# Routing in two rounds through a table in DRAM: a fused attention and mixture-of-experts kernel

## The chip, the core and the metric

The kernel runs on one core of a Trainium2 chip. A core has five engines that run side by side, each through its own queue of instructions in order: PE (TensorE, matrix products into PSUM), DVE (VectorE), ACT (ScalarE), POOL (GpSimd) and SP (SyncE, here only used to issue DMAs). The profile lists PE's weight loads apart, as PEld. The metric is the time of one execution on the device in microseconds (us); lower is better.

## The reference, cut to what matters

`B, H, S, D = 8, 8, 576, 64`; eight experts, model width 512, hidden width 1024, all in f32.

```python
# attention: heads 0-3 see the last 32 positions, heads 4-7 every 32nd position before
scores = where(mask, q @ k.T / sqrt(64), -1e9)
x = softmax(scores) @ v                      # laid out as (B, S, 512)
# mixture of experts, one expert per row
logits = x @ w_gate                          # (B, S, 8)
fresh = argmax(logits); stay = sigmoid(x @ w_local) >= 0.5
for b in range(B):
    for s in range(S):                       # e follows the row before when stay is set
        e = prev_e if (s > 0 and stay[b, s]) else fresh[b, s]
        out[b, s] = softmax(logits[b, s])[e] * (relu(x[b, s] @ w1[e]) @ w2[e])
```

A row can only be put to its expert when its logits are known and the rows before it in its batch have been decided. The order of batches doesn't matter to the result.

## The kernel before

**Attention** (`attention`, L148). The work is cut into 32 pairs of heads (8 batches of 4 pairs, two local and two strided), each pair into two units (`Unit`). One loop, L389, goes over the 64 units: it issues `load` four pairs ahead on SP, `scores` and `mask` of unit n, `values` and `norm` of unit n-2, `store_x` (the finished rows to the DRAM tensor `xd`, by POOL, L305 and L311), `turn_x` of unit n-4, and for the last pair of a batch `logits` and `gates` 5 and 6 units later. `gates` leaves, for each row, its softmax (`probs`) and a code for the expert it picks (`codes`). The order is written out by hand (`manual_schedule`). From unit 12 on the weights of expert 0 are loaded by SP (`Weights.ready`, L577), and from unit 20 on one of 16 sums of weight blocks is formed per unit, by POOL (L582).

**Routing** (`route`, L412) runs once, after all batches. It turns the codes so that each of 64 lines is one (batch, expert), scans along the 576 positions for the expert in force (`last`, L464), counts (`cum`, L472), works out a slot for each row, and then inverts rows to slots by products with one-hot matrices: `at` (L539), `put` (L540 on POOL, L541 on DVE), `lane` (L545) and 96 products into `tab` (L548). From `tab` come `gi` (the row to gather for each slot), `si` (the row to scatter to) and `gate`.

**Experts** (`experts`, L601). Slots come in tiles of 128 rows, up to seven per expert. For every expert in turn two pairs of tiles are always done, and a `Switch` on the count of its tiles runs the rest. A pair is `pair_hidden` (L680, seven products of 16 matmuls, Strassen-like with sums of blocks) and `pair_output` (L716, seven products of 8); `gather` (L629), `scale` (L635), `turn` (L642) and `row_sums` (L651) bring up the next pair while the output of this one is computed; `scatter` (L655) writes the result rows. The weights of expert e+1 are loaded at the start of expert e, and their 16 sums (`steps`) are spread over e's work on DVE.

Of the kernel before, what the change touches and what calls it, by code (L numbers as in the profile page):

```python
# [8 lines left out]
F32 = mybir.dt.float32  # L9
# [9 lines left out]
P = 128  # L19
# [25 lines left out]
NT = E * XT  # L45

AT = (N + E * (P - 1)) // P

# [41 lines left out]
def attention_then_scomoe(ctx: ExitStack, tc: tile.TileContext, qkl, qks, vl, vs, wg, q, k, vl2, vs2, wg2, w1, w2, out):  # L90
# [6 lines left out]
    flag = keep.tile([1, 1], I32, name="flag")  # L97

    with ExitStack() as fast:
        once = fast.enter_context(tc.tile_pool(name="once", bufs=1))  # L100
        gi = once.tile([P, NT], I32, name="gi")
        si = once.tile([P, NT], I32, name="si")
        gate = once.tile([P, NT], F32, name="gate")
        pick = once.tile([1, E], I32, name="pick")
        sums = once.tile([P, 2 * B * PAIRS, 2, 3], F32, name="sums")
        tabs = gi, si, gate, pick, flag
        one = Weights(once)
        with ExitStack() as first:
            routing = first.enter_context(tc.tile_pool(name="routing", bufs=1))
            probs = routing.tile([LQ, LT, B, E], F32, name="probs")  # L110
            codes = routing.tile([LQ, LT, B, E], F32, name="codes")
            with ExitStack() as part:
                with tc.manual_schedule():
                    attention(part, tc, qkl, qks, vl, vs, wg, xd, ident, probs, codes, sums,
                              lambda: one.ready(nc, w1, w2, 0))
            with ExitStack() as part:
                route(part, tc, ident, probs, codes, sums, tabs)
        with ExitStack() as part:
            with tc.manual_schedule():
                experts(part, tc, xd, w1, w2, out, ident, tabs, one)  # L120
# [27 lines left out]
def attention(ctx, tc, qkl, qks, vl, vs, wg, xd, ident, probs, codes, sums, weights):  # L148

    nc = tc.nc  # L150
    consts = ctx.enter_context(tc.tile_pool(name="consts", bufs=1))
# [5 lines left out]
    psS = ctx.enter_context(tc.tile_pool(name="psS", bufs=2, space=PSUM))  # L157
    psV = ctx.enter_context(tc.tile_pool(name="psV", bufs=2, space=PSUM))
    psT = ctx.enter_context(tc.tile_pool(name="psT", bufs=1, space=PSUM))
# [65 lines left out]
    ci = consts.tile([LQ, E], I32, name="ci")  # L225
    nc.gpsimd.iota(ci, pattern=[[-1, E]], base=E, channel_multiplier=0)
    down = consts.tile([LQ, E], F32, name="down")
    nc.vector.tensor_copy(down, ci)
    pi = consts.tile([LQ, LT], I32, name="pi")
    nc.gpsimd.iota(pi, pattern=[[E * LQ, LT]], base=E, channel_multiplier=E)  # L230
    pos8 = consts.tile([LQ, LT], F32, name="pos8")
    nc.vector.tensor_copy(pos8, pi)
    start = consts.tile([LQ, LT], F32, name="start")
# [63 lines left out]
    def store_x(u):  # L297
# [3 lines left out]
        for a in range(2):  # L301
            if u.local:
                w = LQ // 2
                o = dst.rearrange("(t a p) d -> a p t d", a=2, p=w)[a]
                nc.gpsimd.dma_start(out=o, in_=src[a * (P - w):a * (P - w) + w])  # L305
                continue
            for j in range(GT):
# [3 lines left out]
                nc.gpsimd.dma_start(out=o, in_=src[a * (P - w):a * (P - w) + w, j])  # L311
# [39 lines left out]
    def gates(b):  # L351
        ps = psV.tile([P, 2, 3, V1], F32, name="vps").rearrange("p a i e -> p (a i e)")
        lt = ps[0:LQ, 0:LT * (E + 1)].rearrange("p (t e) -> p t e", e=E + 1)
        for t in range(LT):
            nc.tensor.matmul(lt[:, t], lhsT=st["lT", b][:, t * LQ:(t + 1) * LQ], rhs=fold,  # L355
                             start=(t == 0), stop=True, skip_group_check=True)
        lg = lt[:, :, 0:E]
        mx = small.tile([LQ, LT], F32, name="gmx")
        nc.vector.tensor_reduce(mx, lg, axis=AX.X, op=Alu.max)
        mxb = spread(mx, [LQ, LT, E])  # L360
        ex = small.tile([LQ, LT, E], F32, name="ex")
        nc.vector.tensor_tensor(ex, lg, mxb, op=Alu.subtract)

        eq = small.tile([LQ, LT, E], F32, name="eq")
# [22 lines left out]
    for n, u in enumerate(units):  # L387
        u.n = n
# [907 lines left out]
```

## Time and profile before

| | us |
|---|---|
| median of 3 runs (lowest, highest) | 782.3 (781.42, 784.19) |
| the profiled execution: its own time | 780.91 |
| its span | 779.2 |
| PE busy, DVE, ACT, POOL | 707.3, 391.5, 199.1, 173.5 |
| last value product of the attention ends | 167.5 |
| first matmul of the first expert's hidden layer | 239.6 |
| last output scatter ends | 762.6 |

The span is the part of an execution that the profile covers; 1.7 us of the profiled execution's time lie around it. Busy time is the union of an engine's instructions. A row of a group gives the line of the program, the engine, the operation, what it writes and reads, and how often; then the time in total, the mean of one in ns, and idle time of the engine just ahead of it with what ended that idle time. The chain of waits is followed back from the last instruction, at each step to what released it.

### The profile page before, as it was taken

To read this page: it belongs to the slowest core of one execution; us is meant where nothing else is said; L and a number is where in the kernel's file an instruction comes from. 1 tells how busy PE (TensorE), PEld (TensorE's weight loads), DVE (VectorE), ACT (ScalarE), POOL (GpSimd) and SP (SyncE) were. 2 spreads that over 40 slices of the span, in tenths; PEclk is the share of its full clock that TensorE was granted. 3 is DMA by queue.
4 is the path that set the end of the run, shared out by engine and by line. 5 is a ranking of instruction groups with operands and counts; after the bars stand their busy time and mean duration, and the time that the engine had idled before them with its cause. 6 is when DMAs were issued, how large, how long until landed. Compare 5 with 4: busy or idle time off the path is not lost.

```text
span 779.2 us, 15215 instructions
## 1 busy us (share of the span) xinstructions
PE 707.3 (91%) x6244; PEld 638.5 (82%) x6244; DVE 391.5 (50%) x842; ACT 199.1 (26%) x357; POOL 173.5 (22%) x216
## 2 busy tenths in 40 slices
PE   7998899984467999999999999999999999999990
PEld 5887788863467999999899799899989899889990
DVE  6457655537802664366364266466436546333430
ACT  2553344540002222122222222122212222222210
POOL 2346743330210210120121120131012112112101
PEclk9999999995558999999999999999999999999995
DMA  9999678320025110622520712620161432011000
GB/s 332 340 404 306 214 253 268 116 71 1 0 76 196 49 46 18 239 79 76 198 69 30 251 43 60 232 82 29 42 220 55 147 124 70 30 33 56 29 3 23
DMA packets 31639, 95.67 MB, mean 123 GB/s; under 512 B 5614, under 2 KB 5614, under 8 KB 31472
## 3 DMA queue, kind: packets, MB, share of 16 engines
q1 hardware_dynamic: 19424, 64.33, 24.0%
q0 software_dynamic: 11520, 29.39, 11.4%
q8 instruction: 64, 1.05, 0.6%
q14 instruction: 103, 0.84, 0.3%
q10 hardware_dynamic: 528, 0.07, 0.1%
HBM read 74.87 MB, written 19.92 MB: 122 GB/s over the span
## 4 chain that ended last, share of the span: by engine, by line
PE 83%; DVE 6%; issue 5%; ACT 2%; DMA 1%; POOL 1%; ACTq 0%; another core or an unknown queue 0%; POOLq 0%; DVEq 0%
PE mps L716 28%; PE lps L680 28%; PE vps L280 6%; PE sps L256 6%; PE tps L321 3%; PE tab L548 3%; PE xps L642 2%; PE lps L771 2%; PE mps L781 2%; DVE eq L369 1%; PE sps L250 1%; PE tps L340 1%; PE vps L355 1%; DVE put L541 1%; DMA x<-xd,gi 1%
## 5 line engine op out<-in xcount | busy, mean ns | idle before, releaser
L655 POOL DMA_INDIRECT out_dram<-y,si x40 | 47.7, 1192 | 387.2 <-DVE y L668 300.9
L680 PE MATMUL lps<-tt,ws 128*128 128x128 f32 x912 | 108.0, 275 | 0.0
L680 PEld LDWEIGHTS lps<-tt,ws 128*128 128x128 f32 x912 | 104.9, 192 | 0.0
L716 PE MATMUL mps<-wt,k 128*128 128x256 f32 x456 | 101.5, 379 | 0.0
L716 PEld LDWEIGHTS mps<-wt,k 128*128 128x128 f32 x456 | 86.6, 190 | 11.8
L680 PE MATMUL lps<-xt,w1t 128*128 128x128 f32 x608 | 75.5, 278 | 6.1 <-ACT p L687 6.0
L680 PEld LDWEIGHTS lps<-xt,w1t 128*128 128x128 f32 x608 | 73.0, 193 | 9.3 <-ACT p L687 7.5
L716 PE MATMUL mps<-w2t,h 128*128 128x256 f32 x304 | 71.9, 379 | 0.0
L667 ACT ACTIVATE h<-h 128x512 f32<-128x512 f32 x57 | 35.9, 630 | 113.4 <-DVE h L668 113.4
L668 DVE TENSOR_TENSOR h<-lps,u 128x512 f32<-128x512 f32 x57 | 39.4, 691 | 49.9 <-PE lps L680 49.9
L716 PEld LDWEIGHTS mps<-w2t,h 128*128 128x128 f32 x304 | 56.3, 190 | 6.9
L311 POOL DMA_DIRECT2D xd<-xs x80 | 45.7, 576 | 61.4 <-DVE xs L294 47.3
L629 POOL DMA_INDIRECT x<-xd,gi x40 | 39.1, 976 | 85.6 <-issue 39.2
L256 PE MATMUL sps<-qk 64*128 64x96 f32 (+2 forms) x704 | 55.3, 289 | 0.5 <-DMA qk<-in_qkl_dram 0.5
L260 ACT ACTIVATE e<-sps 128x576 f32<-128x576 f32 (+1 forms) x64 | 41.6, 650 | 49.4 <-PE sps L256 49.2
L256 PEld LDWEIGHTS sps<-qk 64*128 64x128 f32 (+2 forms) x704 | 44.7, 188 | 11.1 <-issue 9.3
L668 DVE TENSOR_TENSOR u<-lps,p 128x512 f32<-128x512 f32 x19 | 13.1, 691 | 52.3 <-ACT p L687 20.8
L680 PE MATMUL lps<-tt,w1t 128*128 128x128 f32 x304 | 37.0, 275 | 0.0
L680 PE MATMUL lps<-xt,ws 128*128 128x128 f32 x304 | 37.0, 275 | 0.0
L643 ACT COPY xt<-xps 128x512 f32<-128x512 f32 x40 | 21.7, 589 | 59.6 <-PE xps L642 59.6
L668 DVE TENSOR_TENSOR u<-lps,u 128x512 f32<-128x512 f32 x19 | 13.1, 691 | 45.6 <-PE lps L680 45.6
L716 PE MATMUL mps<-w2t,k 128*128 128x256 f32 x152 | 36.0, 379 | 0.0
(190 smaller groups left out, 1016.7 us busy)
## 6 DMA issues: line engine op xcount, KB each, us to landing
w1t<-in_w_dram SPq DMA_DIRECT2D x8, 2048.0 KB, 17.9
w2t<-in_w_dram SPq DMA_DIRECT2D x8, 2048.0 KB, 11.9
qk<-in_qkl_dram SPq DMA_DIRECT2D x16, 592.0 KB
qk<-in_qks_dram SPq DMA_DIRECT2D x16, 576.0 KB, 7.8
vl<-in_vf_dram SPq DMA_DIRECT2D x8, 780.0 KB, 9.4
vs<-in_vg_dram SPq DMA_DIRECT2D x8, 639.8 KB
xd<-xl POOLq DMA_DIRECT2D x16, 288.0 KB, 6.7
xd<-xs POOLq DMA_DIRECT2D x64, 63.0 KB, 5.6
```

Of the source, the lines that this page charges most:

```text
L256: nc.tensor.matmul(ps[0:m, h, c:c + w], lhsT=t[r, S + j * width:S + j * width + m], rhs=t[r, j * width:j * width + w], start=(u.local and ...
L260: nc.scalar.activation(e[0:kb, :, 0:n], ps[0:kb, :, 0:n], Act.Exp, bias=0.0, scale=1.0 / DH ** 0.5)
L280: nc.tensor.matmul(ps[a * HALF:(a + 1) * HALF, h, i], lhsT=u.e[0:m, h, q0:q0 + HALF], rhs=vt[0:m, j, 2 * i2 + h], start=(i == 0 and h == 0 ...
L311: nc.gpsimd.dma_start(out=o, in_=src[a * (P - w):a * (P - w) + w, j])
L321: nc.tensor.transpose(ps[:, t], src[:, t], ident)
L548: nc.tensor.matmul(tab, lhsT=lane[:, i], rhs=put[:, i], start=(i == 0), stop=(i == CM - 1))
L629: nc.gpsimd.indirect_dma_start(out=r.x[:, i], out_offset=None, in_=xd, in_offset=bass.IndirectOffsetOnAxis(ap=gi[:, j:j + 1], axis=0))
L655: s = nc.gpsimd.indirect_dma_start(out=out, out_offset=bass.IndirectOffsetOnAxis(ap=si[:, j:j + 1], axis=0), in_=y[:, i], in_offset=None, ...
L667: relu = lambda o, i: nc.scalar.activation(o, i, Act.Relu)
L668: add = lambda o, i, p: nc.vector.tensor_tensor(o, p, i, op=Alu.add)
L680: nc.tensor.matmul(ps[:, f], lhsT=m[:, kk, f * P:(f + 1) * P], rhs=v[:, kk], start=(start and f == 0 and kk == 0), stop=(kk == 1), skip_gr ...
L716: nc.tensor.matmul(ps[:, 0:256], lhsT=m[:, f], rhs=v[:, f], start=(start and f == 0), stop=(f == 3), skip_group_check=True)
```

## The change

It does the routing in two rounds of four batches (`RB = 4`), in a class `Router` that replaces `route`:

- Instead of products with one-hot matrices, a row's slot is used as an address: 20 indirect DMAs a round (128 rows each, 64 for every fifth) write pairs of 8 bytes (row number, gate) to a table `T` in DRAM, laid out slot by slot. POOL issues them. `fetch` reads the table back: after round 0 only the first two tiles of experts 0 and 1 (`tab1`), after round 1 all of it (`tab`).
- Round 0 is placed at steps 19 to 24 of the attention. Round 1 is placed among the products of the first pair of expert 0 and the first pair of expert 1, which only take rows of batches 0 to 3 (`floor` lifts the counts of these two experts to 256, so that later rows go to later tiles).
- The order of experts becomes: first pair of 0, first pair of 1, rest of 1, rest of 0, then 2 to 7 as before. The register with an expert's count is loaded at that expert (`choose`), not for all eight ahead.
- The attention's loop goes over pairs of heads, with the scores of a whole pair, then `turn_x` of two pairs back, then the values of the pair before. `store_x` is issued by SP instead of POOL, the weight sums of expert 0 by DVE instead of POOL (two in each of steps 9 to 16). `gates` works on tiles of 128 positions instead of 96.
- The first pair is gathered, scaled and turned at the end of the attention's loop. The pools of the experts are opened with waits for each tile.

The core of the diff: the attention's loop, the steps of a round, the scatters and the table in `Router`, and the beginning of `Experts.run`.

```diff
-    for n in range(len(units) + 7):
...
+    n = PAIRS * RB + 3
+    turn, scan, hot, count, slot, back = router.steps(0, bank)
+    for do in (turn, scan, hot, count, slot, back, *router.scatters(0), lambda: router.fetch(True)):
+        also[n].append(do)
+        n += do in (turn, scan, count, slot, back)
+    also[len(units) - 1] += [lambda: router.table(True), lambda: moe.gather(moe.first)]
+    also[len(units)] += [lambda: moe.scale(moe.first)]
+    for n in range(len(units) + 3):
+        if n < len(units):
+            if n + ahead < len(order):
+                load(*order[n + ahead])
+            if n == 6:
+                steps = moe.W[0].ready(nc, w1=moe.w1, w2=moe.w2, e=0)
+            for u in units[n]:
+                scores(u)
+                mask(u)
+        if 0 <= n - 2 < len(units) and order[n - 2][1] % 2 == 1:
+            store_x(units[n - 2][1])
+        if 0 <= n - 2 < len(units) and n != len(units):
+            turn_x(*order[n - 2])
+        if 0 <= n - 1 < len(units):
+            for u in units[n - 1]:
+                values(u)
+                norm(u)
+        if n == len(units):
+            turn_x(*order[n - 2])
+        elif n == len(units) + 1:
+            moe.turn(moe.first, spare, 0)
+        for do in steps[:2] if n >= 9 else []:
+            do()
+            steps.remove(do)
+        for d, do in ((3, gates), (2, logits)):
+            if 0 <= n - d < len(units) and order[n - d][1] == PAIRS - 1:
+                do(order[n - d][0])
+        if n == len(units) + 1:
+            moe.turn(moe.first, spare, 1)
+            moe.row_sums(moe.first)
+        for do in also[n]:
+            do()
...
+        def turn():
+            for t, c, m in parts:
+                o = ps[0:R, c] if t < last else two[0:R, 0:m]
+                nc.tensor.transpose(o, self.codes[0:m, t, bs].rearrange("p b e -> p (b e)"), ident[0:m, 0:m])
+            nc.scalar.copy(out=self.run[:, 0:last * P], in_=ps[0:R, 0:last * P])
+            nc.scalar.copy(out=self.run[:, last * P:], in_=two[0:R, 0:S - last * P])
+        def scan():
+            nc.vector.tensor_tensor_scan(self.last, self.run, self.run, 0.0, Alu.max, Alu.max)
+        def hot():
+            nc.vector.tensor_scalar(self.last, self.last, E - 1, None, Alu.bitwise_and)
+            nc.vector.tensor_scalar(self.run, self.last, self.er, None, Alu.is_equal)
+        def count():
+            nc.vector.tensor_tensor_scan(self.cum, self.run, self.run, 0.0, Alu.add, Alu.max)
+        def slot():
+            nc.tensor.matmul(ps[0:R, 0:1], lhsT=self.same, rhs=cnt, start=True, stop=True, skip_group_check=True)
+            nc.tensor.matmul(ps[0:R, 1:2], lhsT=self.before, rhs=cnt, start=False, stop=True, skip_group_check=True)
...
+            nc.vector.scalar_tensor_tensor(self.cum, self.cum, self.base, self.run, Alu.add, Alu.mult)
+        def back():
+            for t, c, m in parts:
+                for o in range(0, P, m):
+                    nc.tensor.matmul(ps[o:o + m, t], lhsT=self.cum[:, c], rhs=ident[0:R, 0:R], start=True, stop=True,
+                                     skip_group_check=True)
...
+            nc.vector.tensor_copy(self.tok.bitcast(F32)[:, :, bs, 1], p)
...
+                s = self.nc.gpsimd.indirect_dma_start(
+                    out=self.T, out_offset=bass.IndirectOffsetOnAxis(ap=self.idx[0:m, t, b:b + 1], axis=0),
+                    in_=self.tok[0:m, t, r * RB + b], in_offset=None, bounds_check=P * NT - 1, oob_is_err=False)
+                self.tc.declare_no_dep(s.ins, group="slots", reason="scatters write different slots")
...
+    def fetch(self, early):
+        if early:
+            self.nc.gpsimd.dma_start(out=self.tab1, in_=self.rows(0, 2, EARLY))
+        else:
+            self.nc.gpsimd.dma_start(out=self.tab.rearrange("p (k e) v -> p k e v", e=E), in_=self.rows(0, XT, E))
+    def table(self, early):
+        if early:
+            self.nc.vector.tensor_scalar(self.gi1, self.tab1[:, :, :, 0], RB * S - 1.0, None, Alu.min)
+        else:
+            self.nc.vector.tensor_scalar(self.gi, self.tab[:, :, 0], N - 1.0, None, Alu.min)
...
+        sums = load(1, W[1])
+        other = Rows(spots[1], *self.early, [1, EARLY + 1], RB * S)
+        self.gather(other)
+        todo = router.steps(1, bank)
+        places = slots(todo, [2, 2, 1, 1]) + slots(sums, [2, 2, 2, 1, 1])
+        more = router.scatters(1)
+        for place, n in zip(places[4:], (4, 2, 2, 2, 2)):
+            place += [more.pop(0) for _ in range(n)]
+        output(self.first, W[0], pair_hidden(self.first, W[0], places), other, places)
+        second = rows(0, 1, (2, 3))
+        places = slots(sums, [2, 2, 2, 2])
+        for place in places:
+            place += [more.pop(0) for _ in range(2)]
+        places += [[lambda: router.arms(bank), lambda: router.table(False), lambda: self.gather(second)]]
+        h = pair_hidden(other, W[1], places)
+        router.fetch(False)
+        output(other, W[1], h, second, places)
+        nxt = rows(1, 0, (2, 3))
+        rest(1, W[1], 0, second, choose(1), [], nxt)
```

Between the two small products of `slot` and its last line stand four sums on 32 values; `back` has four DVE steps ahead of the copy into `tok`. A place is run by `pair_hidden` (four places) and `pair_output` (one in `part1`, four in `part2`) between the products. `arms` works out `pick` and the flag: ten small DVE steps, three over all of `sums`, and three small products. The function of `pair_hidden`, `pair_output`, `single`, `turn` and `row_sums` is unchanged.

## The prediction

> **What bounds the kernel now.** I read the slices of the page first: PE is busy nearly throughout, except for one hole.
>
> ```profile
> PE   7998899984467999999999999999999999999990
> DVE  6457655537802664366364266466436546333430
> PEclk9999999995558999999999999999999999999995
> ```
>
> The hole lies between attention and experts, the granted clock there is 0.5, and DVE has its peak in it. The windows of 20 us size it:
>
> ```profile
> 160.00:180.00 20.00, 14.36 (x180) 11.79 (x178) 9.48 (x52) 5.93 (x13) 7.55 (x16) 0.82 0.23 60
> 180.00:200.00 20.00, 5.51 (x34) 4.80 (x34) 17.03 (x41) 0.00 (x0) 2.54 (x1) 0.50 0.00 1
> 200.00:220.00 20.00, 13.98 (x66) 14.01 (x66) 11.55 (x6) 0.00 (x0) 3.06 (x1) 0.50 0.00 0
> 220.00:240.00 20.00, 9.11 (x42) 8.48 (x42) 0.85 (x5) 2.41 (x5) 3.97 (x4) 0.50 0.54 197
> ```
>
> The columns are PE, PEld, DVE, ACT, POOL, clock, DMA share, GB/s. DMA is idle for 40 us: nothing but the routing runs. The chain of waits names its pieces:
>
> ```profile
> 165.35 0.81 PE tps L321 x6
> 166.15 1.32 PE vps L280 x40
> ...
> 198.51 7.38 DVE put L541
> 206.02 20.81 PE tab L548 x96
> ...
> 230.35 6.58 DMA x<-xd,gi
> 236.94 0.72 ACT x L635
> 237.70 2.09 PE xps L642 x8
> ```
>
> The last value product ends at 167.5, the first hidden product starts at 239.6. These 72 us are what the change can reach. A smaller loss lies in the attention. In its timeline:
>
> ```profile
> 59.49 5.05 DVE L369 TENSOR_TENSOR eq<-eq,down 96x48 f32<-96x48 f32 x1
> 59.52 2.51 POOL L582 TENSOR_TENSOR ws<-ws,w1t 128x512 f32<-128x512 f32 x2
> 61.97 2.49 POOL L582 TENSOR_TENSOR ws<-w1t 128x512 f32<-128x512 f32 x2
> 66.75 0.91 PE L280 MATMUL vps<-vs,e 126*64 126x65 f32 x16 [2.69 <-DVE sums L293]
> ```
>
> A DVE step of 0.2 us lasts 5.05 while POOL forms weight sums, and PE waits. It happens again at 82.6.
>
> **The sum, part by part** (against the profiled execution, 780.91 with span 779.2; the median, 782.3, is 1.4 above).
>
> *Weight sums to DVE.* Batches follow each other on PE every 18.9 us (products into vps at L355, 104.2 to 123.1), but take 23.1 to 23.2 across the two stalls: 2 x 4.3 = 8.6 us. Without POOL's sums the stalls have no cause: -8.6. On DVE the 16 sums cost 0.68 each, two a step: 1.4 on local pairs that already need 3.0 (two masks 0.76, two norms 0.76), against some 4.2 to 4.7 of PE per pair. That is just covered; without the cover 8 local steps would lose up to 0.5 each, 0 to 4, taken as 1 together with the next part.
>
> *Stores to SP.* POOL loses 12 issues a batch of 0.58 to 0.64. SP's issues last 0.33, 4 us per 18.9, and loads stand four pairs (19 us) ahead, with queue qk to landing 7.8. Cost 0, behind that lead. If a store holds SP for more than the lead, PE waits for qk; the trace of before shows SP held for 10.4 us once (31.89, behind the weights) without PE waiting.
>
> *Round 0 beside the attention.* PE gets five transposes, two small and six small products: by the rows of cps, nps and hps (0.1 to 0.2 each warm) 1.6 us. DVE gets 1.34 + 0.95 + 1.35 + 0.8 + some 2 of small steps, 6.5 over five steps with 1.5 to 3 free in each: 0. They share one PSUM pair of banks with turn_x: +1 with the above. POOL issues 20 scatters. The nearest row is the gather and scatter:
>
> ```profile
> L655 POOL DMA_INDIRECT out_dram<-y,si x40: 982/1218/1352, 265.1 to 761.7; - x40
> DMA to landing us min/median/max: 2.4/3.3/8.3
> L629 POOL DMA_INDIRECT x<-xd,gi x40: 941/969/1097, 229.0 to 716.5; - x40
> ```
>
> Gathers in a row start 1.27 apart (230.35, 231.63). So 16 x 1.27 + 4 x 1.0 = 24.5 us, from 121 (step 23 ends) to 146; landing, fetch and landing of it end near 152; `table` stands at step 31, near 158. Slack 6 us. Free in my sum; at 1.6 us a scatter or more DVE would wait at `table` with the masks and norms behind it.
>
> Here a rule speaks against the change. The rows: indirect DMAs issued beside DVE's tensor-tensor steps lasted at most 1.35 against 0.94. The Trainium skill ("SBUF — State Buffer", "A bandwidth-pool intuition that's wrong") says that a DMA whose descriptors GpSimd writes took 3.1 us instead of 0.62 beside a DVE copy, since DVE held the port: by it 40 scatters would cost up to 40 x 2.5 = 100 us more, and the change would lose. But its section "Who interferes with whom" gives that to copies, casts and tensor-scalars inside SBUF; what runs beside these scatters are masks, norms and weight sums, tensor-tensors as in my rows. I take the rows.
>
> *The hole closes.* After the last values: turn_x of pair 30 and 31 (0.78 each with a 0.7 copy between), logits 0.6 later, gates 3.0 after the logits start as at 170.5 to 173.55, gates 1.1 warm: 7.3 us, with both turns of the first rows (0.5 each) inside its waits. So hidden products begin at 167.5 - 8.6 + 1.6 + 1 + 7.3 = 168.8 instead of 239.6: -70.8 all told. The first pair took 26.24 at the cold clock against 25.47 for the next: -0.8.
>
> *Round 1 in the first pair* (a product of hidden is 1.79). turn goes in at 3.6, its codes ready by then (gates' DVE chain, 2.3 us). Scan ends near 6.6, the sum u3 near 8.6, hot 9.6, count 11.0; PE is at the slot products at 9.5 and waits 1.5. With 1.65 of own PE work the hidden part lasts 15.8 instead of 12.5: +3.3.
>
> *The table's way back.* POOL starts scatters at 15.8 and is held in order: 8, then y's scatter (result at 27.2), two, y's second, two, then 8 in the second pair: the last is issued near 45 (from the pair's start). Landing 2.4, fetch (896 pieces of 64 bytes, guessed 0.8 from the 0.64 of 288 pieces in L305) and 4 to land: 53. `table` on DVE, gather 1.0 and 3.7 to landing: 57.3, scale 0.7: 58. PE, having begun the second pair at 28.8, would turn these rows at 52.4. DVE stands at `table` from 46.6, with the adds v2 to v4 behind it, and PE behind those. `arms` (13 DVE steps, some 3 us, and small products) comes just ahead of `table` and lies within that wait; with a table in time it would cost PE some 1.5. The pair ends at 61.5 instead of 54.3: +7.2. Of an 8-byte scatter no row shows the landing: not under 1.8 (lowest landing of a store to xd), not over 8.3 (highest of a y scatter); I take 2.4 since little data moves. Only the last scatter's landing counts, so the bounds move the sum by -0.6 to +6. Wait gaps like these cool the clock (0.71 in the window at 65 to 70, after a 2.7 wait): +1.
>
> *The rest.* Row counts by the reference's inputs: experts 0 and 1 have 365 and 249 rows in batches 0 to 3; lifting 249 to 256 leaves expert 1 at 4 tiles, all at 40 as now (40 scatters in the trace). One more tile would be 14 us (7.1 + 6.9 of `single`), excluded by the counts. Weight sums and switches are as before; a switch costs PE 1.6 us over a double pair (52.53 against 2 x 25.47), eight before and after. Register loads move from the idle stage into PE's stream: no row shows one. From below 0[...]; from above 0.82, all that POOL waited ("issue") ahead of its first gather, times 8, 6.6: I take 1.5, nearer nothing. `gates` has six products and the same DVE steps as now, `constants` adds some 20 DVE and POOL steps of 0.2 and a DMA at step 2, where DVE is half free (3.9 busy of 5 at 10 to 15, 2.2 at 15 to 20): 0. The first weight load of expert 1 starts as the attention's buffers free up, and its sums stand 16 us later; 4 MB came within 12 us of 228 (197 GB/s over the last window above): 0.
>
> Sum: -70.8 - 0.8 + 3.3 + 7.2 + 1 + 1.5 = -58.6. Span 720.6, own time 722.3, median 723.7. I say 723.
>
> **Rivals.**
> 1. *The sum above* (0.58): 723.
> 2. *The table is back in time* (0.14): scatters faster than a 128 x 2 KB row's, nothing waits in the second pair: 8.2 less, and the unknown register loads nothing: 713. For it: 8 bytes a row, not 2 KB; against: POOL's time looks set by rows, not bytes (0.64 for 288 KB, 0.58 for 63 KB).
> 3. *POOL is slower per scatter* (0.23): at 1.8 us, 0.53 x 20 = 10.6 later in round 1 and 10.6 - 6 = 4.6 in round 0: 738. For it: y's scatters at 1.22 median, 1.35 highest, beside busy DVE, plus 0.3 between issues.
> 4. *Scatters in a chain* (0.04): each waits for the landing of the one before, as writes to one tensor. Pitch 0.98 + 3.3 or so; each us above 1.27 costs 20 in round 1 and 20 less 6 of slack in round 0. All of the gain (59) is gone at a pitch of 2.9; at 3.6 it is 723 + 47 + 41 = 811. The declared group without dependencies speaks against it, and the y scatters at 265.08 and 267.28 are 2.2 apart where a landing takes 3.3.
> 5. That the hole doesn't close, since W[1] or the expert PSUM banks come free late (0.01): near before.
>
> **How the numbers follow.** Unknown landings and register loads put the first case at 715 to 733. With rivals 2 and 3 the range 708 to 742 leaves out about 0.16. A measurement of this kernel tells some 0.3% (2.4 us). Only rival 4 and the larger part of 5 end above 785: slower 0.04, same 0.01, faster 0.95.
>
> **What would show it.** Right: the half-clock stretch gone; hidden products starting near 169; L369's 5 us gone; scatters 1.3 apart; a PE gap of some 7 us in pieces in the second pair, DVE waiting at `table` for the fetch. Wrong: gaps of PE in the attention at steps 9 to 16 or 31 (sums, table), SP's stores delaying qk, scatters over 1.6 apart, more than 2 us lost at each switch.

## The result: 760.3 us, two fifths of the gain forecast

The changed kernel took 760.27 us (median of 4 runs, 757.6 to 765.78) where the kernel before took 783.25 beside it: ratio 0.971, 95% interval 0.964 to 0.9781. The forecast was 723, range 708 to 742. The profiled execution took 758.07 with a span of 756.3, 35.7 more than the sum's 720.6. In some groups of later runs (a group is run together on one chip) the same program, instruction for instruction, took 727 to 731; what lies between the two is what the experiments are about.

The page's slices of the changed kernel, as it was first measured:

```profile
PE   7999998289798699999999999999999999999993
DVE  6667765035364633573563356365436636424341
PEclk9999998589799999999999999999999999999998
```

Slices are counted from 1. The old hole of half clock, slices 10 to 13, has shrunk to a dip in slice 11. A new one stands at slice 8, earlier, in the middle of the attention, and DVE is at 0 there: it is not a stage in which DVE works alone, as routing was. Slices 13 and 14 also have dents. The windows of 20 us (columns: PE, PEld, DVE, ACT, POOL, clock, DMA share, GB/s):

```profile
100.00:120.00 20.00, 19.36 (x318) 15.88 (x315) 15.08 (x43) 8.60 (x18) 0.00 (x0) 0.93 0.74 261
120.00:140.00 20.00, 12.25 (x153) 10.20 (x153) 4.79 (x14) 3.33 (x6) 11.11 (x12) 0.76 0.73 230
140.00:160.00 20.00, 7.40 (x78) 5.12 (x78) 3.73 (x9) 2.37 (x6) 9.00 (x10) 0.53 0.38 116
160.00:180.00 20.00, 19.72 (x339) 16.33 (x338) 10.87 (x35) 10.45 (x19) 0.00 (x0) 1.00 0.20 54
```

All engines but POOL fall together, for as long as POOL issues round 0's scatters. Intervals between the products of `gates` (L354) of one batch and the next, from PE's instruction starts, are 18.8, 19.4, 18.8, 21.2, **48.5**, 18.8, 17.9 us. Some lines of the timeline of that stretch, with idle time and its end in brackets:

```profile
126.02 1.39 PE L276 MATMUL vps<-vs,e 126*64 126x65 f32 x40
127.33 0.64 PE L252 MATMUL sps<-qk 64*128 64x96 f32 x5
128.38 0.18 DVE L289 RECIPROCAL sums<-vps 128x4 f32<-128x4 f32 x1 [1.37 <-PE vps L276]
129.10 0.47 PE L252 MATMUL sps<-qk 64*128 64x96 f32 x3 [0.29 <-issue]
135.23 0.53 PE L252 MATMUL sps<-qk 64*128 64x96 f32 x2 [1.39 <-issue]
138.30 0.97 POOL L558 DMA_INDIRECT slots<-tok,idx  x1 [0.30 <-issue]
139.58 0.97 POOL L558 DMA_INDIRECT slots<-tok,idx  x1 [0.30 <-issue]
144.45 0.20 DVE L289 RECIPROCAL sums<-vps 128x6 f32<-128x6 f32 x1 [15.43 <-remote]
148.69 0.27 PE L276 MATMUL vps<-vl,e 128*64 128x65 f32 x1 [2.08 <-issue]
151.04 0.27 PE L276 MATMUL vps<-vl,e 128*64 128x65 f32 x1 [2.08 <-issue]
154.72 1.05 PE L276 MATMUL vps<-vl,e 128*64 128x65 f32 x15 [1.14 <-issue]
154.89 1.19 ACT L256 ACTIVATE e<-sps 128x576 f32<-128x576 f32 x2 [28.06 <-remote]
```

POOL keeps its pitch of 1.28. DVE stands 15.4 us before a reciprocal whose value products ended at 127.4 on PE; ACT stands 28.1 before an exponential whose scores ended on PE at 129.6. No instruction that they need is running, so the profile can only write "remote". The signal itself is late: the trace records the one of PE that frees DVE at 144.42, 17 us after the products' end. PE issues single matmuls with 2.1 us of idle time between them and nothing to wait for ("issue"). All go on together at 154.7, some 4 us after the last scatter is done. This is called the stop below.

### The profile page after: what moved, and what is told of

The parts are those of the page before. It is cut to its first block, busy times and chain, and to the rows that moved or that the text cites. A ratio compares the mean times of both kernels' runs of the same rounds, so it can differ in the third digit from the quotient of the medians.

```text
span 756.3 us, 15109 instructions
## 1 busy us (share of the span) xinstructions
PE 691.1 (91%) x6150; PEld 618.2 (82%) x6150; DVE 374.0 (49%) x851; ACT 199.2 (26%) x360; POOL 134.1 (18%) x147
## 4 chain that ended last, share of the span: by engine, by line
PE 80%; issue 6%; DVE 4%; another core or an unknown queue 3%; ACT 2%; DMA 2%; POOL 1%; ACTq 1%; POOLq 0%; DVEq 0%
PE lps L736 28%; PE mps L772 28%; PE vps L276 6%; PE sps L252 5%; PE tps L317 3%; PE lps L827 2%; PE xps L679 2%; PE mps L838 2%; PE sps L246 2%; PE vps L354 1%; PE tps L336 1%; DMA x<-xd,gi 1%; DMA qk<-in_qks_dram 1%; ACT xt L680 1%
## 5 line engine op out<-in xcount | busy, mean ns | idle before, releaser
L692 POOL DMA_INDIRECT out_dram<-y,tab x40 | 45.7, 1141 | 337.5 <-DVE y L724 268.8
L558 POOL DMA_INDIRECT slots<-tok,idx x40 | 40.9, 1023 | 149.3 <-DVE tok L549 137.7
L252 PE MATMUL sps<-qk 64*128 64x96 f32 (+2 forms) x704 | 53.5, 285 | 5.7 <-issue 4.3
L736 PE MATMUL lps<-tt,w1t 128*128 128x128 f32 x304 | 38.7, 282 | 5.5 <-DVE u L724 5.5
L736 PEld LDWEIGHTS lps<-tt,w1t 128*128 128x128 f32 x304 | 36.9, 198 | 5.9 <-DVE u L724 5.9
L276 PE MATMUL vps<-vl,e 128*64 128x65 f32 x768 | 29.4, 235 | 9.4 <-issue 7.3
```

The costliest lines, as they stand in the source:

```text
L252: nc.tensor.matmul(ps[0:m, h, c:c + w], lhsT=t[r, S + j * width:S + j * width + m], rhs=t[r, j * width:j * width + w], start=(u.local and ...
L276: nc.tensor.matmul(ps[a * HALF:(a + 1) * HALF, h, i], lhsT=u.e[0:m, h, q0:q0 + HALF], rhs=vt[0:m, j, 2 * i2 + h], start=(i == 0 and h == 0 ...
L558: s = self.nc.gpsimd.indirect_dma_start(out=self.T, out_offset=bass.IndirectOffsetOnAxis(ap=self.idx[0:m, t, b:b + 1], axis=0), in_=self.t ...
L692: s = self.nc.gpsimd.indirect_dma_start(out=self.out, out_offset=bass.IndirectOffsetOnAxis(ap=r.si[i], axis=0), in_=y[:, i], in_offset=Non ...
L736: nc.tensor.matmul(ps[:, f], lhsT=m[:, kk, f * P:(f + 1) * P], rhs=v[:, kk], start=(start and f == 0 and kk == 0), stop=(kk == 1), skip_gr ...
```

## The experiments

Three readings were open at first: many 8-byte writes to crowded lines of DRAM; any burst of indirect DMAs; or SP's stores beside them.

**First group: bursts in the kernel before, one scatter, scatters spread.** The bursts are eight dummy DMAs each by POOL, behind the masks of units 36, 44 and 52:

```diff
             scores(units[n])
             mask(units[n])
+            if n == 36:
+                burst("dense scatter")       # 8-byte rows, consecutive places; then "sparse scatter", "sparse 512 scatter"
```

> The kernel before, with three bursts of eight indirect scatters by POOL into tables in DRAM that nothing reads, issued one after the other in the attention: at unit 36 rows of 8 bytes whose 1,024 places fill an 8 KB window without a hole, at unit 44 the same rows of 8 bytes at places 512 bytes apart, at unit 52 rows of 512 bytes at places 32 KB apart. Nothing of the kernel's own work is changed. Theory A (a train of small scatters to crowded places holds up the other engines' signals): the first burst stops PE for about the 10 us that POOL needs for it (8 x 1.28), the second and third cost under 1 us, total +10. Theory B (any train of indirect DMAs by POOL does it): all three cost about 10 us each, +30. Theory C (a train of 8-byte rows does it, wherever they go): the first two cost 10, the third under 1, +20. Theory D (it takes SP's stores of x beside the scatters, which the kernel before gives to POOL): none of the three costs over 1 us and no engine shows a wait put down to 'remote'.

> The kernel before with three other bursts of eight DMAs by POOL that nothing needs: at unit 36 the scatters of 8-byte rows to crowded places again, at unit 44 eight plain DMAs of 128 x 8 bytes to consecutive rows, at unit 52 eight indirect gathers of 8-byte rows from the crowded places. If the small packets as such do it, all three stop PE for about 10 us (+30). If it is the list of places that POOL turns into descriptors for small rows, scatters and gathers do and plain DMAs don't (+20). If it is the writes to crowded places in DRAM, scatters and plain DMAs do and gathers don't (+20, the other two). If it takes SP's stores beside them, none does (under +3 in all).

They took 786.5 and 787.2 beside 783.3; every batch interval of the first kernel stayed within 0.1 us of the kernel before, and no engine had a wait put down to remote. In the second the interval from 81 to 108 us was 3.6 us longer, with 2.7 of them ahead of its first burst (104.0); that fits none of the theories. Taken alone, the two speak for SP's stores; but these executions had no stop, as the later groups show, so they settle nothing.

```diff
-    for do in (turn, scan, hot, count, slot, back, *router.scatters(0), lambda: router.fetch(True)):
+    for do in (turn, scan, hot, count, slot, back, router.scatters(0)[0], lambda: router.fetch(True)):
```

> The changed kernel with one of the 20 scatters of round 0 instead of 20; the tokens of the other 19 are left out of the table, so most rows of batches 0 to 3 are not computed. If the scatters hold the attention up, the batch with them, which took 48.5 us from one L354 to the next where its neighbours take 18.8 to 19.4, takes about 19 to 20, and the first hidden product starts near 172 instead of 201.7. If the stop comes from round 0's other work in the same place (its PE products back to 128 partitions, the fetch of the table, the stores on SP), the batch stays above 40 and the first hidden product near 200.

```diff
+    for i, do in enumerate(router.scatters(0)):
+        also[n + i // 4].append(do)
+    also[n + 5].append(lambda: router.fetch(True))
```

> The changed kernel with round 0's 20 scatters issued four at each of the steps 24 to 28 instead of all at one step; the fetch of the table follows at step 29. If what holds the engines up is the length of the train (descriptors or signals that pile up behind it), trains of four cost little: the batches with them take 20 to 22 us, the stop shrinks from 29.7 us to under 8, and the time is 725 to 738. If each scatter costs the other engines its 1.3 us wherever it stands, the 20 still cost some 25 us, now over two batches, and the time stays within 2 per cent of the changed kernel's 760. If the scatters are innocent, the time stays there too, and the stop stays where the fetch or the stores are.

One scatter (most rows of the result are then missing): 730.5 us, interval 21.7. Spread: 730.95 (726.74 to 739.45), ratio 0.9364, interval 0.9291 to 0.9436, batch interval 21.2. It looked as if the train's length was shown. It wasn't: POOL has nothing between the scatters in either listing, so it issued them at the same times as in the changed kernel (125.4 to 151.2), and every engine's instructions and waits are in the same order in both. The spread version *is* the changed kernel to the chip.

**Second group: the same program again.** The first kernel is the changed kernel, the second its spread listing with unchanged line numbers.

> The changed kernel itself, line for line, once more. Set beside the version with the scatters spread over five steps, each engine has the same instructions in the same order with the same waits (POOL has nothing between the scatters in either), and POOL issues the 20 scatters from 125.4 to 151 us in both; yet one took 760 and the other 731. If the stop belongs to the program as it stands, this run takes 755 to 766 again, with PE nearly still from 127 to 155 us and the first hidden product near 201. If the stop belongs to the circumstances of that execution (where the program and its tables lay, or what else the chip did), this run takes 725 to 740, the batch with the scatters 21 to 22 us, and the first hidden product starts near 171.

> The changed kernel with round 0's scatters listed four to a step over five steps, with the same line numbers as the changed kernel; each engine's instructions, order and waits are the same as the changed kernel's. If this listing is what matters, it takes 727 to 739 whatever the changed kernel takes beside it. If nothing of the listing matters, it takes what the changed kernel takes beside it on the same chip, within 1 per cent.

768.47 (762.51 to 772.57) and 760.75 (759.12 to 770.42), ratios 0.9788 and 0.9739, both with the stop (12.64 and 6.53 us of PE in the windows 120:140 and 140:160 of the first). So one instruction stream takes 731 in one group and 761 in another, with the four runs of a group within 2% of each other, and the kernel before takes 783 in both. The stop belongs to the circumstances, and what brings it on has still to be in the program, since only this program has it.

**Third group.** The changed kernel, the burst kernels, and a table with its rows 64 bytes apart:

```diff
-        self.T = dram.tile([P * NT, 2], I32, name="slots")
+        self.T = dram.tile([P * NT * 8, 2], I32, name="slots")
...
-            nc.vector.tensor_scalar(idx, s, float(E), -1.0, Alu.mult, Alu.add)
+            nc.vector.tensor_scalar(idx, s, 8.0 * E, -8.0, Alu.mult, Alu.add)
```

> The changed kernel again, unchanged, on whatever chip this group of runs is given: the first two measurements of it (760, 768) and one of the same instruction streams (761) were on one chip, the one that took 731 on another. If the chip decides, this is near 731 or near 762 to 768, with a stop of 26 to 30 us in the fifth batch interval only in the second case; the three other kernels of this group run beside it on the same chip and are read against it. If it changes from one loading to the next, it can be either, whatever the chip.

> The kernel before with bursts of eight indirect scatters by POOL again (8-byte rows to crowded places at unit 36, 8-byte rows 512 bytes apart at unit 44, 512-byte rows at unit 52). In the first group none cost anything, but those ran on a chip where the 20 scatters of the changed kernel cost nothing either. If the kernel beside it shows the stop: theory A (crowded 8-byte writes) expects 5 to 10 us in the batch of the first burst and none in the others; theory C (small rows) 5 to 10 in the first two; theory B (any burst of indirect DMAs) in all three; theory D (only beside SP's stores) in none. If the kernel beside it shows no stop, all are under 1 us again and this tells nothing.

> The kernel before with eight scatters of 8-byte rows to crowded places (unit 36), eight plain DMAs of 128 x 8 bytes (unit 44) and eight gathers of 8-byte rows (unit 52). If the kernel beside it shows the stop: writes of 8 bytes to crowded places as the cause give 5 to 10 us at units 36 and 44 and none at 52; descriptors made by POOL from a list give it at 36 and 52; small packets as such at all three. In the first group the total rose by 4 us with a late stretch between 81 and 127 us, which would come again.

> The changed kernel with the table's rows 64 bytes apart instead of 8 (index times 8, table eight times as large, and seven DMAs for the whole table and two for the early part, where one did each). The scatters are the same 20, of 8 bytes a row at the same pitch. If many 8-byte writes into the same lines of DRAM hold up the rest of the chip, the stop of round 0 (26 to 30 us where the changed kernel beside it has it) shrinks below 5; if it is the number of small packets or of scatters, it stays above 20. The seven DMAs of the last fetch cost up to 8 us later in either case.

No stop here: 726.55, 785.3, 794.3 and 748.0, so nothing was told apart (of the 8 us that the second burst kernel lost, 3 lie ahead of its first burst at 103.7 and 5 between 115 and 165, beside its bursts; nothing there is put down to remote, and the cause is not known). But the group gives the changed kernel's profile without the stop, on the very chip that had shown it before:

```profile
PE   7999999997997999999999998999999899999993
DVE  6568767553674327536533573664365465323431
```
```profile
120.00:140.00 20.00, 19.72 (x342) 16.54 (x339) 11.95 (x39) 9.26 (x17) 12.82 (x13) 1.00 0.84 252
140.00:160.00 20.00, 19.40 (x350) 16.13 (x344) 11.81 (x38) 9.07 (x17) 7.91 (x8) 1.00 0.67 188
```

The same 20 scatters (POOL 12.82 and 7.91 busy, against 11.11 and 9.00) with PE at 342 and 350 matmuls instead of 153 and 78.

**Fourth group: bursts of other kinds, with the mark beside them.** From here on the bursts stand in the changed kernel, whose own round 0 is the mark: it tells whether the stop is there. They queue on POOL, which is idle, and so run one after the other from 19.7 us on.

```diff
+    for n, kind in [(8, 'dense gather'), (12, 'plain'), (16, 'sparse scatter'), (20, 'sparse 512 scatter')]:
+        also[n].append(lambda kind=kind: router.burst(kind))      # ten DMAs each
```

> The changed kernel with four bursts of ten DMAs by POOL that nothing needs, each in a batch of its own ahead of round 0: gathers of 8-byte rows from consecutive places (step 8), plain DMAs of 128 x 8 bytes (step 12), scatters of 8-byte rows to places 512 bytes apart (step 16), scatters of 512-byte rows to places 32 KB apart (step 20); the 20 scatters of round 0 follow at step 24 as they are and show whether this execution has the stop at all. The changed kernel has taken 760, 768 and 761 us in two groups of measurements and 727 to 731 in two others, so this can be either. If round 0 stops PE (interval to the next L354 near 48 us): any burst of DMAs with many small packets as the cause gives 8 to 15 us in all four intervals before (where 18.8 to 21.2 is the plain value); scatters of 8-byte rows alone give it at step 16 only; rows to crowded places alone in none of the four; indirect DMAs alone in three, not at step 12. If round 0 does not stop PE, all intervals stay within 2 us.

> The changed kernel with the table's rows 64 bytes apart, again; it took 748 in a group in which the changed kernel itself took 727, with no stop in either. If this group is one with the stop and crowded places in DRAM are its cause, the interval of round 0 is 20 to 22 us here while the kernel beside it shows 48; if not, it is 45 to 50 in both, and the time is near 780. Without the stop it is 748 again.

808.0 and 776.6; round 0's intervals were 46.9 and 46.6, so the stop was there. The wide table's window holds 20 scatters and 81 matmuls, where the same kernel had 477 in the third group:

```profile
138.00:165.00 27.00, 8.06 (x81) 6.53 (x80) 2.79 (x6) 1.26 (x3) 19.30 (x20) 0.59 0.54 180
```

Crowded places in DRAM are out. The bursts, by windows that hold them: gathers (19 to 32), plain DMAs (32 to 37.8), 8-byte scatters (42 to 55), 512-byte scatters (55 to 68):

```profile
19.00:32.00 13.00, 6.86 (x93) 5.21 (x87) 2.96 (x18) 1.43 (x3) 9.53 (x11) 0.77 0.83 285
32.00:42.00 10.00, 8.76 (x107) 7.46 (x106) 4.24 (x10) 3.02 (x6) 5.38 (x10) 0.62 0.18 59
42.00:55.00 13.00, 7.49 (x75) 3.95 (x74) 2.18 (x4) 1.59 (x4) 9.96 (x10) 0.80 0.54 168
55.00:68.00 13.00, 4.11 (x10) 2.09 (x10) 0.00 (x0) 0.00 (x0) 9.82 (x10) 0.50 1.01 389
```

Gathers, small scatters and larger scatters all stop PE (10 matmuls in the last 13 us). Set against the first measurement matmul by matmul (PE's 6150 run in the same order in both), PE fell back by 9.6 us from 21 to 33, by 3 from 33 to 39, by 0.3 from 39 to 42, and by 27 from there to 78. The ten plain DMAs cost at most those 3 us, which lie in the 6 us right behind the gathers and may be theirs. Whether SP's stores have to be beside the train was not separated; only the bursts in the kernel before, whose stores go by POOL, could have shown it, and both of their groups had no stop.

**Fifth to seventh group: pitch and length.** Memsets on POOL (0.46 us) after each scatter set the pitch.

```diff
+    def fill(self, n):
+        for _ in range(n):
+            self.nc.gpsimd.memset(self.good, 0.0)
```

> The changed kernel with four bursts of eight scatters of 8-byte rows by POOL (512 bytes apart, nothing reads them) from about 20 us on, set apart by 8 us of memsets on POOL: one after the other, then with one, three and six memsets of 0.46 us after each scatter (pitch 1.3, 1.8, 2.7 and 4.1 us if POOL is free). Round 0's own 20 follow. Where the execution has the stop: if each indirect DMA holds the other engines for as long as POOL works at it, each burst costs PE about the same 6 to 10 us whatever its pitch. If it is the train, a queue that only clears when POOL pauses, the first costs about 10, the second less, the third and fourth under 1. Where it hasn't, none costs over 1 us and round 0's interval is 20 to 22 us.

> The changed kernel with four other bursts by POOL from about 20 us on, set apart by 8 us of memsets: two scatters of 8-byte rows, four of them, eight plain DMAs of 128 x 8 bytes, eight gathers of 512-byte rows of w1. Where the execution has the stop: if an indirect DMA costs the others its own time, PE loses some 2, 4, 0 and 8 us; if the stop builds up with the train's length, under 0.5, under 2, 0 and 8; if writes to DRAM are what stops it, the gathers cost nothing; if small packets do, the plain DMAs cost 3 to 5 and the gathers nothing.

> The changed kernel with bursts of scatters of 8-byte rows by POOL that nothing reads, from about 18 us on, set apart by 8 us of memsets: two one after the other, then eight with one memset after each (pitch 1.6 us, as measured), eight with three (2.7), seven with six (4.1); round 0's own 20 at pitch 1.3 follow and tell whether the stop is there. If it is (interval to the next L354 near 47): a price of each indirect DMA gives PE the same loss of some 1 us for each scatter in every burst (2, 8, 8, 7); a train that clears only when POOL pauses gives under 1, some 8, under 2 and none. If it isn't, each burst costs at most 1.5 us, which the memsets cost in the group before.

733.98, 738.98 and 737.83, round 0's intervals 21.7, 23.3 and 20.4: none had the stop, so these three tell nothing of it. The second shows an ordinary cost: beside its gathers of w1 the load of expert 0's weights lands late, the chain names it for 17.75 us up to 57.4, and PE behind DVE's sums fell back by 9 us. The next run carried a burst at full pitch as its mark:

```diff
+    for what in [('scatter', 8, 0, 16), ('scatter', 8, 1, 16), ('scatter', 8, 3, 16), ('scatter', 7, 6, 0)]:
+        also[8].append(lambda what=what: router.burst(*what, moe))    # kind, number, memsets after each, at the end
...
                 self.tc.add_to_no_dep_group("slots", s.ins)
+                self.fill(2 - 2 * r)
```

> The changed kernel with the four bursts of scatters that nothing reads at pitches of 1.3, 1.6, 2.7 and 4.1 us (eight, eight, eight and seven, from about 18 us on, 8 us of memsets between them), and with two memsets after each scatter of round 0 (pitch 2.1 us, 42 us in all from about 125). The first burst is the mark: PE loses some 6 to 12 us in it if this execution has the stop, and under 1.5 if not. With the stop, a price of each indirect DMA gives about the same loss in the second, third and fourth burst, and some 20 to 28 us in round 0; a train that needs POOL without a pause gives some 6 to 8, under 2 and 0, and under 8 in round 0. Without it all four are under 1.6 us, and round 0's later table alone costs some 10 us at the end of the attention.

762.7, with the stop. The windows of the bursts at 1.28 us (13.9 to 24.2), 1.57 (32 to 44), 2.66 (52 to 72) and 4.1 (81 to 108):

```profile
14.00:24.00 10.00, 8.75 (x94) 6.72 (x90) 1.73 (x5) 1.94 (x3) 7.87 (x8) 0.63 0.97 354
32.00:44.00 12.00, 9.06 (x142) 7.30 (x138) 4.24 (x10) 1.98 (x5) 10.75 (x15) 0.91 0.44 157
52.00:74.00 22.00, 20.42 (x371) 17.14 (x367) 12.94 (x40) 9.43 (x18) 18.50 (x35) 1.00 1.00 376
81.00:110.00 29.00, 27.69 (x487) 22.64 (x486) 22.41 (x59) 14.02 (x28) 24.93 (x48) 1.00 0.88 308
```

and the first two of the execution without the stop:

```profile
14.00:24.00 10.00, 10.00 (x164) 8.14 (x163) 4.82 (x25) 3.89 (x6) 0.00 (x0) 0.90 0.99 361
32.00:44.00 12.00, 11.72 (x194) 9.58 (x187) 5.65 (x23) 5.30 (x9) 0.00 (x0) 1.00 0.66 218
```

Matmul by matmul against that execution, which is the third group's, with the 8 us behind each burst counted to it. The last column has the same for executions that had no stop: the first kernel of the fifth group, the version with pauses below, and the spread listing.

| scatters, pitch (us) | PE falls back by (us) | without the stop |
|---|---|---|
| 8 at 1.28 | 8.4 | 0.4 |
| 8 at 1.57 | 7.5 | 1.5 |
| 8 at 2.66 | 1.4 | 1.1 |
| 7 at 4.1 (8 without the stop) | 0.3 | 3.3 |
| 20 at 2.17 (round 0, up to 183 us) | 5.3 | 2.4 |
| 20 at 1.28 (round 0 of the changed kernel) | 27 | 0.7 |

So it is no price of each indirect DMA. A train whose scatters (0.98 us of POOL each) stand 1.7 us apart costs no more than without the stop, at 1.2 us some 3 us more in 20, at 0.3 or 0.6 it holds everybody up. One execution stands behind most of these rows, and the bursts lie beside different work.

The pitch is not all. Round 1 begins with eight scatters with 0.3 us between them (219.8 to 231.1 in the changed kernel as first measured), and PE loses nothing in any of the seven traces with the stop. The train of 14 behind them, y's scatters counted, stops it from about its sixth on; in round 0 PE's first gap stands at the third. Round 0 runs beside loads (144 GB/s) and many short products, those eight beside 1 GB/s and long products. Whether length or what runs beside it decides was not separated.

**Two marks in the traces** tell the circumstances apart. Waits put down to remote stand in all seven traces of the changed kernel and its variants with the stop, and in none of the eight without. The trace also records the signals of DMAs that have landed. For the eight harmless scatters of round 1 every trace without the stop has 128 records, 16 for each; those with it have 59 to 75, though nothing waits there. Between 120 and 160 us the changed kernel has 176 with the stop (first measurement) and 728 without. So signals, or only their records, go missing too. Every execution on record has a span and a granted clock, so none is known to have run unrecorded; whether the recording has a part in the stop was not tested. Loads of instructions by DMA show nothing: the packets begun inside the stop (126 to 147) took 0.7 to 1.4 us each, the median of the larger ones being 1.0.

**A version with pauses in round 0** (two memsets after each scatter, pitch 2.17; the steps ahead closed up to start one step sooner):

```diff
-        n += do in (turn, scan, count, slot, back)
+        n += do in (turn, count, slot, back)
...
+                for _ in range(2 - 2 * r):
+                    self.nc.gpsimd.memset(self.good, 0.0)
```

> A version: the changed kernel with two memsets on POOL after each scatter of round 0 (pitch 2.1 us, 42 us in all), and the steps ahead of them closed up so that they start one step of attention sooner (some 118.5 us). Without the stop: the table comes back near 163 where DVE asks for it at 160, and two scans and what lies between them share a step, so 3 to 6 us more than the changed kernel's 727: 730 to 733. With the stop: if it is a train that a pause of 0.9 us clears, 740 to 750 where the changed kernel has 760 to 770 (round 1's trains stay as they are and still stop, some 12 us); if each scatter has its price, 765 to 775.

> The version with two memsets after each scatter of round 0 again; it took 738 in a group without the stop. There again if this group has none. If it has, pauses of 0.9 us leave 5 us of loss in 20 scatters by the run before (where the trains at full pitch lose 28), and round 1's trains, which stay at full pitch, lose some 10: about 750 to 756, where the changed kernel has 760 to 770. If the pauses don't help, 770 to 780.

First 738.26 (733.15 to 739.99, ratio 0.9403, interval 0.9351 to 0.9455), without a sign of the stop; more than the 730 to 733 expected, since PE waits 3.5 us for the counts where two scans share a step. Then 746.04 (744.04 to 753.26, ratio 0.9531, 0.9471 to 0.9591), with the stop and below the 750 to 756 expected. The stop shows in round 1's train (a PE gap of 6.7 us up to 231.9) and not in round 0:

```profile
125.00:150.00 25.00, 24.53 (x399) 20.55 (x399) 12.93 (x40) 10.95 (x21) 20.91 (x35) 0.90 0.80 238
```

Across groups, the version is 14 to 22 us ahead of the changed kernel (760 to 768) where the stop is there and 7 to 12 behind it (727 to 731) where it isn't. The unchanged listing remains the fastest that was run, the paced one varies less.

## Why the prediction failed, point by point

The stages by PE's first matmul of each, all from the span's start:

| stage | predicted | as measured first | without the stop |
|---|---|---|---|
| last value product of the attention ends | 161.5 | 190.1 | 161.0 |
| first hidden product of the experts | 168.8 | 201.7 | 173.4 |
| first pair | 28.8 | 31.2 | 31.1 |
| second pair | 32.7 | 39.1 | 31.1 |
| from there to the end of the span | 490.3 | 484.3 | 489.3 |
| span | 720.6 | 756.3 | 724.8 |

The second row includes the first. The 35.7 us over the sum are 28.6 in the attention, 4.3 from there to the experts, 2.4 and 6.4 in the two pairs, less 6.0 in the rest. Why the rest is 5 shorter with the stop than without is not known.

- **The step that failed is "Round 0 beside the attention: free in my sum".** Its own numbers held: pitch 1.28 (1.27 forecast), begun at 125.5 (121) and done by 150.7 (146), the fetch issued at 152. What I costed was POOL's time and the table's due time, so I counted the wait of those who need the scatters. The cost fell on engines that need nothing from them: their batch took 48.5 us, where it takes 20.4 without the stop, so 28 us. The trace of before could not show it, as its longest row of indirect DMAs in a train of pitch under 1.7 had five; I had priced 20 in a row by the duration of one. The rule that I weighed and set aside, the Trainium skill's DMA slowed by DVE copies ("SBUF — State Buffer", "A bandwidth-pool intuition that's wrong"), was not what happened: the scatters kept their median of 0.97 us.

```profile
L558 POOL DMA_INDIRECT slots<-tok,idx x40: 913/974/1499, 125.5 to 249.4; - x40
```

  My ground for setting it aside was half of what the page says, though: its section "Who interferes with whom" also has a tensor-tensor step of DVE with both inputs in SBUF contend with GpSimd's reads. The trace agrees in kind: the two longest scatters, 1.40 and 1.50 us (222.4 and 224.1), lie beside DVE's sums. It is half a us each and explains nothing of the 28.
- **Right in kind:** the hole has shrunk, and the attention without the stop ends within 0.5 of the sum; L369 lasts 0.2 in all eight batches (it had a maximum of 5.05). Of the half-clock stretch between attention and experts some 8 us are left (without the stop 0.62 from 165 to 170, then 0.50 to the first hidden product), where there were some 60.
- **A smaller step that failed: from the last value product to the experts**, 7.3 in the sum, 12.4 without the stop (11.6 with it). The first rows were to fit inside the waits of this stretch. But ACT takes its instructions in order and waits for those rows, while a copy that PE needs queues behind them (lines of the trace without the stop):

```profile
163.84 0.72 ACT L672 ACTIVATE x<-x,tab 128x512 f32<-128x512 f32 x1 [1.41 <-DMA x<-xd,gi]
165.86 0.72 ACT L672 ACTIVATE x<-x,tab 128x512 f32<-128x512 f32 x1 [1.30 <-DMA x<-xd,gi]
166.48 0.68 ACT L321 COPY xT<-tps 128x504 f32<-128x504 f32 x2
167.22 2.15 PE L336 MATMUL tps<-xT,wgs 128*32 128x504 f32 x16 [1.95 <-ACT xT L321]
171.23 2.19 PE L354 MATMUL vps<-fold,lT 128*128 128x9 f32 x12 [0.81 <-DVE lT L344]
```

  The logits (L336) start 6.2 us after the last value product where the sum has some 3, the products of `gates` 4.0 later instead of 3.0, and these last 2.1 instead of 1.1 at the low clock.
- **Round 1 in the first pair** took 31.1 without the stop and 31.2 with it, 2.3 over the sum. PE waits 1.4 for the counts at the slot products (from 213.3, L523), where 1.5 was forecast. The sum took the cold clock for gone (-0.8), but without the stop the first hidden product took 3.34 us at a granted clock of 0.67, where 1.79 was reckoned. PE's own work took 2.1 instead of 1.65, and products just behind it 1.9 to 2.0. (The prediction's own terms give 15.65 for this hidden part and not 15.8; nothing hangs on it.)
- **The table's way back** is the step that came nearest. Without the stop both pairs end 62.2 us after the first hidden product, where 61.5 was worked out. That is partly luck: the first pair took 2.3 more and the second 1.6 less than in the sum. The chain of waits without the stop goes as told, with a shorter landing of the fetch:

```profile
219.76 1.05 POOL slots L558
220.81 0.30 issue
221.12 2.02 DMA slots<-tok,idx
...
223.68 2.80 DMA tab<-slots
...
228.84 3.66 DMA x<-xd,gi
232.52 0.73 ACT x L672
```

  With the stop the second pair took 8 us more, and its chain names the cause as in round 0:

```profile
238.88 0.69 DVE wt L632
239.56 7.40 another core or an unknown queue
246.96 0.02 issue
246.98 0.70 DVE u L724
```

- **Rivals.** The second (the table in time) is refuted even without the stop, where the second pair takes 31.1 and not some 25. The third (POOL slower per scatter) gave 738 and lay nearest in time, but its cause is refuted: POOL was no slower. The fourth (scatters in a chain) is refuted by the pitch. None said that the other engines would be held.
- **The range** counted POOL's pitch, landings and register loads as the unknowns. An operation that the trace of before doesn't show in that number, beside all other engines, was the larger unknown, and its range had nothing for it.

What stays open: what puts an execution into one circumstance or the other (all runs of a group agreed, one chip showed both, and the kernel before took 780 to 787 in all groups), by what path POOL's train holds up the signals and the issue of the others, whether the recording takes part, and whether it needs SP's stores beside it.

## What to carry to other kernels

A queue's own time is not all that a long train of instructions on it can cost: when a change puts many more of one kind in a row than the profile of before ever had, bound the cost to the engines that do not depend on them too. Before an explanation by "spread out" or "reordered" is believed, compare what each engine really executes: two listings can be one program, and a difference between them is then the circumstances'. Where the circumstances can differ, put a mark into the experiment itself, as the burst at full pitch, so that one run says both whether the effect is there and what changes it.

## What the runs showed of the hardware

- In some executions, a train of POOL's indirect DMAs at a pitch of 1.3 to 1.6 us held up the other engines, gathers and scatters alike, 8 or 512 bytes a row: waits for signals of work done long before lasted up to 28 us, and PE issued single matmuls with 2.1 us between them. At 2.7 and 4.1 us it cost no more than in executions without the stop. POOL itself kept its pitch. The first eight scatters of round 1, at 1.2 to 1.8 beside the experts' products, cost nothing.
- In other executions of the same program the same train cost nothing (round 0's batch 20.4 us instead of 48.5).
- With the stop the traces hold 59 to 75 records of landings for eight scatters, without it 128.
- Ten plain DMAs of 8 bytes a row by POOL, 0.6 us apart, cost at most 3 us there.
